# A layer-norm, MLP and memory-recurrence kernel: transposes moved to DMA, the end of the MLP by tiles, two more segments' loads on ScalarE, six last stores

## The chip, the cores and the metric

One NeuronCore of a Trainium2 chip runs the whole program. The metric is the device time of one execution in microseconds; lower is better. TensorE does the matrix products, VectorE and ScalarE the elementwise work, GpSimd some copies, and SyncE, ScalarE and GpSimd issue DMAs.

## The reference

The input `x` has 2048 rows of 1024 bfloat16. It is normalised by rows, and the output is the sum of three things: `x`, a recurrent attention over the normalised rows, and an MLP of the normalised rows.

```python
xn = _layernorm(x, axis=-1)
return x + _A_ref(xn, A_mem0, A_Wq, A_Wk, A_Wv, A_Wo, A_seg_len) + _B_ref(xn, B_w1, B_b1, B_w2, B_b2)

def _B_ref(x, w1, b1, w2, b2):             # w1 1024 x 3584, w2 3584 x 1024
    return gelu(x @ w1 + b1) @ w2 + b2

def _A_ref(x, mem0, Wq, Wk, Wv, Wo, seg_len):   # 32 heads of 128; 64 segments of 32 rows; 8 memory rows
    mem = mem0
    for s in range(n_seg):
        h = jnp.concatenate([mem, xs], axis=1)          # 40 rows
        q, k, v = h @ Wq, h @ Wk, h @ Wv
        p = softmax(where(mask, q @ k.T * scale, -1e9))
        o = (p @ v) @ Wo
        mem = o[:, :M, :]                               # the next segment starts from these rows
        outs.append(o[:, M:, :])
```

The segments depend on one another through the memory rows, so they run in order.

## The kernel before

The program has two stages. The first is the MLP, over four groups of four tiles of 128 rows (`for tg in range(4)`, line 544). The second is the recurrence, over 64 segments (`for s in range(NSEG)`). The order of all instructions is written out by hand: each engine runs its own in the order of the text, and so does each queue of DMAs. The framework adds semaphore waits. It gives the DMAs issued by SyncE and ScalarE eight completion semaphores in turn, and each such DMA waits until the one eight places before it in the program has landed.

**A group of the MLP.** The first product (`first_product`, line 495, matmuls at line 497) makes 28 blocks of 128 hidden columns for the 512 rows of the group from the turned, normalised rows `xnT` (two halves of 512 columns); ScalarE and VectorE apply the gelu and write `gts`. Then, for the first three groups, the `x` tiles of the next group are loaded (`load_x`, line 339), their statistics taken on VectorE (`ln_stats`, line 388, instructions at lines 384 and 386), and a loop over the group's four tiles (line 610) does for each: normalise one tile of the next group (`ln_apply`, line 401, two buffers `ln_xn`), the second product in two halves of 512 columns (28 matmuls each, line 618), two additions on VectorE for each half (lines 625 and 626), the turning of the normalised tile (`turn_x`: eight transposes on TensorE at line 412, two copies out of PSUM at line 417, one on VectorE, one on ScalarE), and the store of the finished tile of `x + MLP` to `R_n` in DRAM (`keep_R`, line 445, on SyncE; on ScalarE for the last four tiles).

After the loop, `keep_xT` (line 427) stores the turned rows for the recurrence (`rows_d`, `rowsL_d`) and has GpSimd copy parts of them, and `turn_R` (line 457, issues at line 484) rearranges `R_n` into `res_d` and `resL_d` by some 56 small DMAs in DRAM, on SyncE for groups 0 and 1, on GpSimd for group 2.

In group 0, between the loads of `x` and the statistics, SyncE also copies 15 of the recurrence's streamed weight units (512 KB each) from the inputs to DRAM scratch (`copies`, by `fetch`, lines 246 and 248) and loads five resident units (`fetch_resident(*EARLY)`).

The last group needs no next one. Its second product runs with all eight results in PSUM: for each of 28 steps `fc`, four tiles by two halves (line 651). Each result starts from a one-row product that adds `b2` (line 644) and a product with the identity that adds `x` (line 645). Slabs that the steps set free get weight units of the recurrence (`fetch_resident`). Eight evictions follow (line 665), four on VectorE and four on ScalarE, and the stores of `R_n`.

**A segment of the recurrence.** Keys, queries and values come from 8 weight units each and half, 48 units, and the output from 16 (`o_product`, line 1027). Of the 64 units of 512 KB, 17 are streamed for each segment through six slabs by SyncE (15 from DRAM, two kept in PSUM), the others stay in SBUF. `put_mem` (line 307) writes the new memory rows into the next segment's input; its VectorE copy at line 324 runs once a segment and marks its end here. The small loads of a segment (its rows, line 286; its residual, lines 1124 and 1150) and the plain stores of its output (line 1218) are on the engine called `loads`:

```python
EARLY_SEGS = 5
loads = nc.scalar if s < EARLY_SEGS else nc.gpsimd
```

In segments 1 to 4 `turn_R` of the last four tiles is put on a list, `small`, of GpSimd DMAs, one or two of which are issued whenever a streamed unit is done. In every fourth segment and the last (`left_o`) the output covers 32 rows more and there are two residual tiles, `res` and `st["resL"]` (in `pd_main`). In the last segment VectorE adds the output to both (line 1184) and twelve stores go out (line 1207), half on SyncE and half on ScalarE.

Of the kernel before, what the change touches and what calls it, by code (L numbers as in the profile page):

```python
# [14 lines left out]
ALU = mybir.AluOpType  # L15
PSUM = bass.MemoryType.PSUM

P = 128
# [6 lines left out]
SEG = 32  # L25
# [3 lines left out]
FC = F // P  # L29
# [8 lines left out]
NX = 24  # L38
NL = SEG - NX
# [9 lines left out]
SCRATCH = 320  # L49
SMALL = 3776  # L50
LEAD = 6
EARLY_SEGS = 5
LEAD_FIRST = 4
SCORES_0 = (6, 6, 6, 5)
SUMS_0 = (4, 4, 4, 4)
# [59 lines left out]
def kernel(  # L115
# [16 lines left out]
    nc = tc.nc  # L132
# [198 lines left out]
    with tc.tile_pool(name="ma", bufs=2) as ma, tc.tile_pool(name="mps", bufs=6, space=PSUM) as mps:  # L331
# [90 lines left out]
        def turn_x(tt, xn, xnT):  # L422
            pT = turned(xn)
            for half in range(2):
                turned_out(tt, pT, half, xnT, nc.scalar.copy if (tt + half) % 2 else nc.vector.tensor_copy)

        def keep_xT(tg, xnT):
            xl = [t[:, 0:512].rearrange("p (g k i t) -> p g k i t", g=2, k=KT, i=GRP) for t in ko_flat]
            for half in range(2):
                nc.sync.dma_start(  # L430
                    out=rows_d[16 * tg:16 * tg + 16, :, 128 * half:128 * half + 128].rearrange("s p c -> p s c"),
                    in_=xnT[half].rearrange("p s k t -> p s (k t)"),
                )
                for g in range(4):
                    nc.gpsimd.tensor_copy(
                        out=xl[g // 2][:, g % 2, 4 * half:4 * half + 4, :, :],
                        in_=xnT[half][:, 4 * g:4 * g + 4, :, NX:SEG].rearrange("p i k t -> p k i t"),
                    )
            for k in range(2):
                nc.sync.dma_start(  # L440
                    out=rowsL_d[4 * tg + 2 * k:4 * tg + 2 * k + 2, :, :].rearrange("g p c -> p g c"),
                    in_=xl[k][:, :, :, :, :].rearrange("p g k i t -> p g (k i t)"),
                )

        def keep_R(ttg, rsb):
            eng = nc.scalar if ttg >= NT - 4 else nc.sync
            eng.dma_start(out=R_n[ttg * P:ttg * P + P, :], in_=rsb[:, :])

        def main_row(slot):
# [94 lines left out]
        for tg in range(4):  # L544
# [53 lines left out]
            if not last:  # L598
                xnT = new_xnT(tg + 1)
                for t in range(4):  # L600
                    xtoks[4 * tg + 4 + t] = load_x(4 * tg + 4 + t)
                if tg == 0:
                    for unit, c in copies.items():
                        fetch(c, unit)
                    fetch_resident(*EARLY)
                for t in range(4):
                    ln_stats(4 * tg + 4 + t)
                ln_sqrt(4 * tg + 4, 4 * tg + 8)
                ln_rstd(4 * tg + 4, 4 * tg + 8)
                for t in range(4):  # L610
                    ttg = 4 * tg + t
                    xn = ln_apply(ttg + 4)
                    rsb = xtoks[ttg]
                    for nb in range(2):
                        cs = slice(nb * 512, (nb + 1) * 512)
                        ps = mps.tile([P, 512], F32, name="ps")
                        for fc in range(FC):
                            nc.tensor.matmul(  # L618
                                ps[:, :],
                                lhsT=gts[fc // 4][:, fc % 4, t * P:(t + 1) * P],  # L620
                                rhs=w2_sb[fc // 2][:, fc % 2, cs],
                                start=(fc == 0),
                                stop=(fc == FC - 1),
                            )
                        nc.vector.tensor_tensor(out=ps[:, :], in0=ps[:, :], in1=b2bc[:, cs], op=ALU.add)
                        nc.vector.tensor_tensor(out=rsb[:, cs], in0=ps[:, :], in1=rsb[:, cs], op=ALU.add)
                        if nb == 1:
                            turn_x(ttg + 4, xn, xnT)
                    keep_R(ttg, rsb)
                keep_xT(tg + 1, xnT)  # L630
                for t in range(4):
                    turn_R(4 * tg + t, nc.gpsimd if tg == 2 else nc.sync)
            else:


                start_stream("xn2")
                start_stream("xn3")
                put_mem(o_sb, nxt["hT"], mps.tile([P, 512], F32, name="ps"), wide=False)
                nc.sync.dma_start(out=d_oL[:, 0:DM], in_=Wo_v[:, h + 1, :])
                pss = [mps.tile([P, 512], F32, name="ps") for _ in range(6)]  # L640
                pss += [mps.tile([P, 512], F32, name="pT", bufs=2) for _ in range(2)]
                for n in range(8):
                    cs = slice((n % 2) * 512, (n % 2 + 1) * 512)
                    nc.tensor.matmul(pss[n][:, :], lhsT=ones[0:1, :], rhs=b2row[0:1, cs], start=True, stop=False)
                    nc.tensor.matmul(
                        pss[n][:, :], lhsT=ident, rhs=xtoks[4 * tg + n // 2][:, cs], start=False, stop=False
                    )
                for fc in range(FC):
                    for t in range(4):
                        for nb in range(2):  # L650
                            nc.tensor.matmul(  # L651
                                pss[2 * t + nb][:, :],
                                lhsT=gts[fc // 4][:, fc % 4, t * P:(t + 1) * P],
                                rhs=w2_sb[fc // 2][:, fc % 2, nb * 512:nb * 512 + 512],
                                start=False,
                                stop=(fc == FC - 1),
                            )
# [16 lines left out]
    with tc.tile_pool(name="late", bufs=1) as late, \  # L674
# [67 lines left out]
        for s in range(NSEG):  # L742
# [435 lines left out]
            for w, r in reversed(list(enumerate(tiles))):  # L1178
                if left_o:
                    o = psX[:, 256 * w:256 * w + 256].rearrange("p (h e) -> p h e", e=32)  # L1180
                else:
                    o = o_sb[:, 0:8, :]
                r_rows = r.rearrange("p (h e) -> p h e", e=32)
                nc.vector.tensor_tensor(out=r_rows, in0=o, in1=r_rows, op=ALU.add)  # L1184
# [11 lines left out]
            if final:  # L1196
                engines = [nc.sync, nc.scalar]
                n = 0
                for w, r in enumerate(tiles):
                    for b in range(2):  # L1200
                        cs = slice(256 * (2 * b + w), 256 * (2 * b + w) + 256)
                        pieces = [(rows, slice(64 * b + m0, 64 * b + m0 + NX))]
                        for sl, row in left_rows:
                            p0 = 64 * b + NL * sl
                            pieces.append((slice(row, row + NL), slice(p0, p0 + NL)))
                        for o, i in pieces:
                            engines[n % 2].dma_start(out=out_flat[o, cs], in_=r[i, :])
# [48 lines left out]
```

## Time and profile before

| | us |
|---|---|
| median of 3 runs | 1818.26 (1816.41 to 4332.87) |
| the profiled execution, its own time | 1811.68 |
| its span, first to last instruction | 1809.9 |
| TensorE busy | 1707.1 |
| VectorE busy | 978.1 |
| ScalarE busy | 687.9 |
| GpSimd busy | 305.2 |
| mean granted TensorE clock | 0.998 |
| MLP, up to the first matmul of the recurrence | 417.0 |
| bytes moved by DMA | 592.07 MB |

The span is one execution, taken by the profiler; times in the text are counted from its first instruction. A group's line on the page gives how often an instruction ran, its busy time in sum, the mean of one in nanoseconds, and the idle time of its engine just before it with what ended that. The chain of waits is followed back from the last instruction, at each step to what released it. In the timeline an entry merges equal instructions that follow one another; a DMA issue on a queue (SPq, ACTq) includes what it waits for. A window's line gives its length, the busy time and number of instructions of TensorE's matmuls, its weight loads, VectorE, ScalarE and GpSimd, and then the granted clock, the DMA engines' share and GB/s.

### The profile page before, as it was taken

The numbers are of one execution on the slowest core, as the hardware profiler recorded it, in microseconds if no ns is written. First come the engines' busy times: TensorE is split into PE (matmuls) and PEld (weight loads), VectorE is DVE, ScalarE is ACT, GpSimd is POOL, SyncE is SP. The second block draws the span as 40 slices with busy tenths as digits, with TensorE's granted clock in tenths as the row PEclk, the third lists the DMA queues.
The fourth block names the chain that finished last, engine by engine and source line by source line (L and its number), as shares of the span: only waits on it lengthen the run. The fifth ranks groups of instructions, "written<-read, shape, count | busy, mean of one in ns | idle before, by whom it ended". The sixth has DMA issues, their size and how long they took to land.

```text
span 1809.9 us, 71522 instructions
## 1 busy us (share of the span) xinstructions
PE 1707.1 (94%) x31173; PEld 893.0 (49%) x31173; DVE 978.1 (54%) x2508; ACT 687.9 (38%) x1700; POOL 305.2 (17%) x595
## 2 busy tenths in 40 slices
PE   8999999998988999999999999999999999999997
PEld 4444444444444545545444555554545454555544
DVE  7657483804554555555555555555555555555554
ACT  6334260702333334333333334343433333434333
POOL 0000000411122211111111212111111111111111
PEclk9999999999999999999999999999999999999999
DMA  9931111769999999999999999999999999999997
GB/s 290 308 100 48 52 48 36 246 225 345 385 371 346 389 377 384 387 377 393 380 373 374 383 395 394 368 398 379 393 385 376 382 370 369 398 393 384 391 396 294
DMA packets 220870, 592.07 MB, mean 327 GB/s; under 512 B 46283, under 2 KB 75995, under 8 KB 220556
## 3 DMA queue, kind: packets, MB, share of 16 engines
q1 hardware_dynamic: 197652, 567.08, 83.5%
q0 software_dynamic: 17184, 17.23, 2.9%
q8 instruction: 244, 4.00, 0.9%
q10 hardware_dynamic: 5720, 3.19, 0.6%
q14 instruction: 70, 0.57, 0.1%
HBM read 573.43 MB, written 28.90 MB: 333 GB/s over the span
## 4 chain that ended last, share of the span: by engine, by line
PE 72%; DMA 13%; issue 6%; ACT 4%; DVE 3%; POOL 1%; ACTq 0%; DVEq 0%; POOLq 0%; SPq 0%
PE acc L769 34%; PE acc L1027 12%; PE ps L497 11%; PE ps L618 8%; DMA u<-Wc_O 7%; DMA u<-Wc_V 3%; PE ps L651 2%; ACT mixed L938 2%; PE acc L978 1%; DMA u<-Wc_Q 1%; PE mixed L886 1%; DVE kq L853 1%; DVE pd_main L951 1%; POOL res_d L486 1%; ACT kq L848 1%
## 5 line engine op out<-in xcount | busy, mean ns | idle before, releaser
L769 PE MATMUL acc<-u,hr_home 128*32 128x512 bf16 x11520 | 760.8, 380 | 15.7 <-issue 6.0
L769 PEld LDWEIGHTS <-hr_home 128*32 128x32 bf16 x12288 | 348.0, 96 | 285.5 <-issue 33.8
L769 PE MATMUL acc<-u,hrL 128*32 128x512 bf16 x2880 | 254.5, 380 | 4.4 <-issue 2.4
L497 PE MATMUL ps<-u 128*128 128x512 bf16 (+1 forms) x920 | 194.4, 373 | 2.0 <-ACT u L417 2.0
L267 DVE TENSOR_SCALAR u<-kept 128x512 uint32<-128x512 uint32 x254 | 163.1, 684 | 51.7 <-PE acc L769 39.2
L821 ACT CAST d_oL<-acc 128x512 bf16<-128x512 f32 x143 | 82.0, 585 | 261.0 <-PE acc L769 254.2
L618 PE MATMUL ps<-u 128*128 128x512 bf16 x672 | 147.0, 379 | 0.0
L1027 PEld LDWEIGHTS <-kq 128*32 128x32 bf16 x3908 | 103.1, 96 | 79.0 <-issue 22.2
L1027 PE MATMUL acc<-u,d_oL 128*32 128x512 bf16 x1944 | 133.9, 381 | 8.5 <-DMA u<-Wc_O 4.7
L497 PEld LDWEIGHTS <-u 128*128 128x128 bf16 x920 | 89.8, 98 | 104.9 <-issue 2.4
L1027 PE MATMUL acc<-u,kq 128*32 128x256 bf16 (+1 forms) x2372 | 117.2, 313 | 16.0 <-DMA u<-Wc_O 13.4
L853 DVE STREAM_TRANSPOSE kq<-kq 128x512 bf16<-128x512 bf16 x128 | 91.0, 711 | 74.8 <-ACT kq L848 72.6
L951 DVE TENSOR_TENSOR pd_main<-kq,mixed 128x320 bf16<-128x320 bf16 x128 | 62.4, 487 | 127.3 <-ACT mixed L938 127.3
L848 ACT CAST kq<-acc 128x512 bf16<-128x512 f32 (+2 forms) x192 | 85.3, 444 | 114.7 <-PE acc L769 85.1
L1218 POOL DMA_DIRECT2D out_dram<-hr_home x172 | 87.2, 514 | 227.3 <-DVE hr_home L1184 226.8
L825 ACT CAST kq<-acc 128x512 bf16<-128x512 f32 x128 | 75.2, 587 | 111.2 <-PE mixed L892 109.9
L769 PEld LDWEIGHTS <-hrL 128*32 128x32 bf16 x3072 | 86.3, 96 | 58.1 <-issue 5.9
L916 DVE TENSOR_TENSOR kq<-kq,mixed 128x96 bf16<-128x96 bf16 (+1 forms) x256 | 38.1, 190 | 125.7 <-ACT kq L906 70.5
L618 PEld LDWEIGHTS <-u 128*128 128x128 bf16 x672 | 65.3, 98 | 77.4 <-DVE g_u L579 0.4
L571 ACT ACTIVATE g_xb<-ps,b1col 128x512 bf16<-128x512 f32 x112 | 76.8, 686 | 55.6 <-PE ps L497 54.7
L938 ACT ACTIVATE mixed<-mixed,small_consts 128x160 f32<-128x160 f32 x256 | 94.2, 368 | 8.4
L1027 PEld LDWEIGHTS <-d_oL 128*32 128x32 bf16 x2592 | 63.8, 96 | 63.8 <-issue 16.1
(132 smaller groups left out, 2015.4 us busy)
## 6 DMA issues: line engine op xcount, KB each, us to landing
u<-Wc_K SPq DMA_DIRECT2D x256, 512.0 KB
u<-Wc_V SPq DMA_DIRECT2D x256, 512.0 KB
u<-Wc_O SPq DMA_DIRECT2D x256, 512.0 KB
u<-Wc_Q SPq DMA_DIRECT2D x192, 512.0 KB
u<-in_B_w_dram SPq DMA_DIRECT2D x28, 512.0 KB
u<-in_A_Wq_dram SPq DMA_DIRECT2D x13, 512.0 KB
u<-in_A_Wv_dram SPq DMA_DIRECT2D x12, 512.0 KB
u<-in_A_Wk_dram SPq DMA_DIRECT2D x9, 512.0 KB
```

Of the source, the lines that this page charges most:

```text
L267: nc.vector.tensor_single_scalar(out=out, in_=in_, scalar=0, op=ALU.bitwise_or)
L497: nc.tensor.matmul(ps[:, SEG * s0:SEG * s1].rearrange("p (s t) -> p s t", t=SEG), lhsT=w1_sb[fb // 2][:, kt, (fb % 2) * P:(fb % 2 + 1) * P ...
L571: nc.scalar.activation(out=xb[:, :], in_=ps[:, :], func=ACT.Identity, bias=b1col[:, fb:fb + 1], scale=1.0)
L618: nc.tensor.matmul(ps[:, :], lhsT=gts[fc // 4][:, fc % 4, t * P:(t + 1) * P], rhs=w2_sb[fc // 2][:, fc % 2, cs], start=(fc == 0), stop=(fc ...
L769: nc.tensor.matmul(o, lhsT=lhs[:, i, :], rhs=m, start=(i == seq[0]), stop=(i == seq[-1]), tile_position=(0, 32 * j),)
L821: cp(out=out, in_=ps.rearrange("p (h e) -> p h e", e=32))
L848: nc.scalar.copy(out=q_home[:, h0:h1, NL:40], in_=ps[:, 32 * h0:32 * h1].rearrange("p (h e) -> p h e", e=32))
L853: nc.vector.transpose(out=home, in_=home)
L938: nc.scalar.activation(out=mixed[:, 160 * b:160 * b + 160], in_=mixed[:, 0:160], func=ACT.Exp, scale=-1.0, bias=off[:, b:b + 1],)
L951: nc.vector.tensor_tensor(out=pdA.rearrange("p c b q -> p b c q"), in0=prA[:, None, :, :].to_broadcast([P, 2, 4, 40]), in1=dd, op=ALU.mult,)
L1027: nc.tensor.matmul(acc[r0:r0 + rows, 0:256 * len(blocks)], lhsT=lhsT, skip_group_check=True, rhs=o_columns(t, k, blocks), start=start, sto ...
L1218: loads.dma_start(out=out_flat[rows, 256 * j:256 * j + 256], in_=res[32 * j:32 * j + NX, :])
```

## The change

It has five parts.

- Tiles 1 to 3 of each next group are turned by DMA: `send_x` issues eight DMA transposes a tile on SyncE, of 32 rows by 512 columns each, straight from `ln_xn` into `xnT`, ahead of the tile's second product. Tile 0 is still turned by TensorE, after its second product.
- The stores of `R_n` for tiles 0 to 2 of a group go to ScalarE. The copies of the streamed units and the five early loads of group 0 stand behind the loop over the tiles on SyncE.
- In the last group the left half of each result no longer gets `x` by a product with the identity; VectorE adds it at the eviction. The last four of the 28 steps run tile by tile.
- `EARLY_SEGS` is 7: segments 5 and 6 have their small loads and plain stores on ScalarE.
- In the last segment the two sums are written side by side into `d_oL`, and six stores of 512 columns take the place of twelve of 256.

```diff
-EARLY_SEGS = 5
+EARLY_SEGS = 7
...
+        def send_x(t, xn, xnT):
+            for i in range(4):
+                for half in range(2):
+                    nc.sync.dma_start_transpose(
+                        out=xnT[half][:, 4 * t + i, :, :],
+                        in_=xn[SEG * i:SEG * i + SEG, 512 * half:512 * half + 512],
+                    )
...
         def keep_R(ttg, rsb):
-            eng = nc.scalar if ttg >= NT - 4 else nc.sync
+            eng = nc.scalar if ttg >= NT - 4 or ttg % 4 < 3 else nc.sync
...
                 for t in range(4):
                     xtoks[4 * tg + 4 + t] = load_x(4 * tg + 4 + t)
-                if tg == 0:
-                    for unit, c in copies.items():
-                        fetch(c, unit)
-                    fetch_resident(*EARLY)
...
                     xn = ln_apply(ttg + 4)
+                    if t > 0:
+                        send_x(t, xn, xnT)
...
-                        if nb == 1:
+                        if nb == 1 and t == 0:
                             turn_x(ttg + 4, xn, xnT)
                     keep_R(ttg, rsb)
+                if tg == 0:
+                    for unit, c in copies.items():
+                        fetch(c, unit)
+                    fetch_resident(*EARLY)
                 keep_xT(tg + 1, xnT)
...
-                    nc.tensor.matmul(
-                        pss[n][:, :], lhsT=ident, rhs=xtoks[4 * tg + n // 2][:, cs], start=False, stop=False
-                    )
-                for fc in range(FC):
-                    for t in range(4):
-                        for nb in range(2):
+                    if n % 2:
+                        nc.tensor.matmul(
+                            pss[n][:, :], lhsT=ident, rhs=xtoks[4 * tg + n // 2][:, cs], start=False, stop=False
+                        )
+                steps = [(fc, t) for fc in range(FC - 4) for t in range(4)]
+                steps += [(fc, t) for t in range(4) for fc in range(FC - 4, FC)]
+                for fc, t in steps:
+                    for nb in range(2):
...
-                    if fc % 2:
+                    if t == 3 and fc % 2:
                         fetch_resident(f"w2_{fc // 2}")
-                    if fc % 4 == 3:
+                    if t == 3 and fc % 4 == 3:
                         fetch_resident(f"gT{fc // 4}")
...
-                    cp = nc.scalar.copy if n % 2 else nc.vector.tensor_copy
-                    cp(out=xtoks[4 * tg + n // 2][:, cs], in_=pss[n][:, :])
+                    x = xtoks[4 * tg + n // 2][:, cs]
+                    if n % 2:
+                        nc.scalar.copy(out=x, in_=pss[n][:, :])
+                    else:
+                        nc.vector.tensor_tensor(out=x, in0=pss[n][:, :], in1=x, op=ALU.add)
...
-                nc.vector.tensor_tensor(out=r_rows, in0=o, in1=r_rows, op=ALU.add)
+                to = d_oL[:, 256 * w:256 * w + 256].rearrange("p (h e) -> p h e", e=32) if final else r_rows
+                nc.vector.tensor_tensor(out=to, in0=o, in1=r_rows, op=ALU.add)
...
-                for w, r in enumerate(tiles):
-                    for b in range(2):
-                        cs = slice(256 * (2 * b + w), 256 * (2 * b + w) + 256)
+                for b in range(2):
+                    cs = slice(512 * b, 512 * b + 512)
...
-                        for o, i in pieces:
-                            engines[n % 2].dma_start(out=out_flat[o, cs], in_=r[i, :])
-                            n += 1
+                    for o, i in pieces:
+                        engines[n % 2].dma_start(out=out_flat[o, cs], in_=d_oL[i, 0:512])
+                        n += 1
```

More of the change, by code (lines that the diff above doesn't have):

```diff
@@ L644 @@
                     nc.tensor.matmul(pss[n][:, :], lhsT=ones[0:1, :], rhs=b2row[0:1, cs], start=True, stop=False)
-                    nc.tensor.matmul(
-                        pss[n][:, :], lhsT=ident, rhs=xtoks[4 * tg + n // 2][:, cs], start=False, stop=False
-                    )
-                for fc in range(FC):
-                    for t in range(4):
-                        for nb in range(2):
[L651 to L657, printed above, removed]
-                    if fc % 2:
+                    if n % 2:
[6 more added lines that the diff above has]
+                    for nb in range(2):
+                        nc.tensor.matmul(
+                            pss[2 * t + nb][:, :],
+                            lhsT=gts[fc // 4][:, fc % 4, t * P:(t + 1) * P],
+                            rhs=w2_sb[fc // 2][:, fc % 2, nb * 512:nb * 512 + 512],
+                            start=False,
+                            stop=(fc == FC - 1),
+                        )
+                    if t == 3 and fc % 2:
                         fetch_resident(f"w2_{fc // 2}")
-                    if fc % 4 == 3:
+                    if t == 3 and fc % 4 == 3:
                         fetch_resident(f"gT{fc // 4}")
@@ L1198 @@
                 n = 0
-                for w, r in enumerate(tiles):
-                    for b in range(2):
-                        cs = slice(256 * (2 * b + w), 256 * (2 * b + w) + 256)
[L1202 to L1205, printed above, removed]
-                        for o, i in pieces:
-                            engines[n % 2].dma_start(out=out_flat[o, cs], in_=r[i, :])
-                            n += 1
+                for b in range(2):
+                    cs = slice(512 * b, 512 * b + 512)
+                    pieces = [(rows, slice(64 * b + m0, 64 * b + m0 + NX))]
+                    for sl, row in left_rows:
+                        p0 = 64 * b + NL * sl
+                        pieces.append((slice(row, row + NL), slice(p0, p0 + NL)))
+                    for o, i in pieces:
+                        engines[n % 2].dma_start(out=out_flat[o, cs], in_=d_oL[i, 0:512])
+                        n += 1
             elif left_o:
```

## The prediction

> **What bounds the kernel now.** I read the page first, then the chain of waits over the first 430 us, then SyncE's queue beside VectorE's timeline around the second token group, then the chain and the windows around 565 us, and the tail. The engine rows and the DMA row of the page:
>
> ```profile
> PE 1707.1 (94%) x31173; PEld 893.0 (49%) x31173; DVE 978.1 (54%) x2508; ACT 687.9 (38%) x1700; POOL 305.2 (17%) x595
> ...
> DMA  9931111769999999999999999999999999999997
> ```
>
> TensorE is busy 94% of the span. The DMA engines are full from the tenth slice on (the recurrence) and nearly idle from the fourth to the seventh (most of the MLP). So in the MLP, which the change mostly edits, TensorE alone should set the time, and only its gaps and extra work can be saved. The chain of waits, second token group:
>
> ```profile
> 161.86 12.09 PE ps L618 x56
> 173.94 0.45 PE pT L412 x8
> ...
> 211.54 0.46 PE pT L412 x8
> ...
> 212.03 0.59 ACT u L417
> ...
> 212.66 48.51 PE ps L497 x224
> ```
>
> A tile's second product takes 12.09 us, its eight transposes 0.45 us; at the end of a group the transposes and ScalarE's copy lie between the last product (211.54) and the next group's first (212.66), 1.12 us. SyncE's queue, where the change rearranges most:
>
> ```profile
> 58.91 2.71 SPq L246 DMA_DIRECT2D Wc_O<-in_A_Wo_dram  x4
> ...
> 83.80 2.65 SPq L248 DMA_DIRECT2D u<-in_A_Wk_dram  x2
> 87.60 26.44 SPq L447 DMA_DIRECT2D R_n<-u  x4
> 114.13 2.55 SPq L430 DMA_DIRECT2D rows_d<-u  x2
> ...
> 155.58 1.87 SPq L344 DMA_DIRECT2D u<-in_A_x_dram  x4
> ```
>
> The 20 half-megabyte issues (15 weight copies in DRAM, 5 loads) hold SyncE from 58.91 to 87.54, 28.6 us, in time when it has nothing urgent. After the group, rows_d and the 56 small DMAs of turn_R fill it from 114.13 until it reaches the x loads of the third group at 155.58. VectorE takes these x tiles up soon after:
>
> ```profile
> 164.92 1.28 DVE L384 BATCH_NORM_STATS2 ln_stats<-u 128x6 f32<-128x512 bf16 x2
> ...
> 171.20 0.55 DVE L403 TENSOR_SCALAR ln_xn<-u,ln_mv,ln_rstd 128x1024 bf16<-128x1024 bf16 x1
> ```
>
> and TensorE transposes the result at 173.94. That chain has only some 9 us to spare. In the recurrence, segment 6 (from the write of its memory rows at line 324 to the next) takes 25.64 us, where later segments of its kind (10, 14, 18, 22) take 20.0 to 21.3. The chain and two windows:
>
> ```profile
> 561.01 1.24 DMA hr_home<-res_d
> 562.25 5.07 DMA pd_main<-resL_d
> ...
> 567.75 0.41 DVE hr_home L1184
> ```
> ```profile
> 564.00:568.00 4.00, 1.17 (x24) 0.34 (x16) 0.59 (x2) 0.00 (x0) 0.00 (x0) 1.00 0.86 328
> 568.00:572.00 4.00, 3.64 (x46) 1.65 (x50) 2.53 (x6) 1.17 (x2) 1.09 (x2) 0.73 0.60 170
> ```
>
> GpSimd, behind its small DMAs, issues segment 5's residual loads late (562.25, 0.7 us before the memory write; in segment 9 it is 6.1 us before); TensorE idles 3.05 us and then runs 3.4 us at half clock. The tail on SyncE:
>
> ```profile
> 1804.46 1.10 SPq L1207 DMA_DIRECT2D out_dram<-hr_home  x3
> 1805.97 1.42 SPq L1207 DMA_DIRECT2D out_dram<-pd_main  x3
> ```
>
> **The change part by part.** *Transposes by DMA.* In each of three groups, tiles 1 to 3 lose 8 TensorE transposes: 6 inner tiles x 0.45 = 2.7 us, and 3 group ends x 1.12 = 3.36 us, together 6.0 us. The copies out of PSUM that also go (9 of 0.59 us on ScalarE, 9 of 0.41 on VectorE) were hidden except at the group ends. In their place stand 24 DMA transposes a group on SyncE, each 32x512. For the last tile they can be issued once VectorE has finished the tile before (two adds of 0.7 us) and the normalisation (0.55), 2.1 us into a product of 12.09; so 10 us remain for eight issues and a landing. The trace has no DMA transpose. The nearest rows are other small SyncE DMAs, 0.6 us of issue: 8 x 0.6 + 2 for the landing = 6.8 us, hidden. The other bound is the pace at which the DRAM copies land, 1.83 us each (SyncE's waits from 64.6 to 90.2, 14 copies). I take the near row: -6.0 us; the far bound is a rival. The Trainium skill (VectorE: DVE Perf Modes, The three transpose paths) gives 1309 ns for a 128x128 crossbar transpose by DMA, the same number of elements, and so speaks against this edit: my estimate from it is 10.5 us for eight, 2.5 us late at each of three ends, 7.5 us more in the sum. No run here shows it yet.
>
> *Stores of R_n on ScalarE.* Nine issues of 0.36 us, each waiting for VectorE's last add of its tile. Behind them on ScalarE stands nothing until the next group's first activation, 12 us after the third: free. GpSimd's copies of the transposed rows stay hidden in the first product.
>
> *The copies and early loads behind the loop.* Their data is needed only after 313 us, so they cost nothing themselves. What stands behind them on SyncE does: rows_d, turn_R, then the third group's x loads. They now start at the last R_n store, some 0.6 us ahead of the old rows_d, and each waits, as the built program has it, for the landing of the DMA eight places before it. At the measured 28.6 us for the block, the x issue goes from 155.58 - 0.9 to 183.3. From there: 2.4 us to the first tile, then VectorE's 6.8 us from the first statistics (164.92) to the normalised tile (171.75), so 192.5. TensorE, running 2.0 us earlier by then (two transposed tiles and one group end), finishes tile 0 at 171.9 and next in its order stand the eight transposes of tile 0 of the next group, which are still on TensorE. It stalls 20.6 us. Afterwards the clock: after the 3.05 us gap above it lost 1.7 us, at the kernel's start 2.8; I take 2.0. Sum +22.6. Bounds: were only issue time to count (15 x 0.6 + 5 x 0.33 = 10.7 us), the stall would be 2.7 us without clock loss; if rows_d and the first turn_R also wait behind the last landings, 24 + 3. I take the measured block, since the eight-deep waits are unchanged. Only the third group's loads are hit: the second's are ahead of the copies, the fourth's have no copies ahead.
>
> *Last group.* Four x matmuls go; a pair there takes 0.64 us: -1.3 us. At 365 us the clock is halved for 3.4 us (loss 1.7), after the slow one-row matmuls; with a shorter stretch I count half: -0.8 (bounds 0 and -1.7). The tile-by-tile end lets six of eight evictions finish early, but the first recurrence product waits for the last ScalarE and VectorE eviction: 1.16 us idle before, about 0.8 after (0.7 of eviction plus 0.1), -0.35. The half-megabyte fetch into the slab freed by step 25 is issued 2.6 us later; DMA share is 0.61 from 415 to 420, so 0.3 (up to 1.3).
>
> *Loads of segments 5 and 6 on ScalarE.* They leave GpSimd's backlog. Segment 6 should fall from 25.64 to the 20.3 or so of its kind: -5; ScalarE gets three and six issues more, and a landing took 6.3 us on that queue in segment 1, so I take -4.5 (bounds -5.3 and +3, if the issues delay the evictions TensorE waits for).
>
> *Six stores.* Three issues less on SyncE, whose last now ends at 1805.6 instead of 1807.4: -1.6 (0 to -2).
>
> Sum: 22.6 - 6.0 - 2.1 - 0.35 + 0.3 - 4.5 - 1.6 = +8.4 us. The profiled execution took 1811.68 us (span 1809.9 and 1.8 around it), so 1820.1; the runs' median, 1818.26, lies 6.6 above it, so I predict 1826.7.
>
> **Rivals.** (1) *No stall, faster.* If the copies, starting into empty DMA engines, leave SyncE after little more than issue time, the x issue is at 165.4 and the stall 2.7 us: -11.5, so 1806.8. It decides from an x issue before about 163 (no stall at all, 1804). For it: the copies met a backlog at 58.9. Against: nine of them issued at once there, and only then the waits of 1.4 to 3 us began. (2) *Transposes late, slower.* At 1.83 us each, 24 take 44 us against a window of 36; the last lands near 122 where the group ends at 111: 11 us late, three times, +33 on top: 1860. Against: 32 KB each, a sixteenth of the copies' bytes. (3) *Segments 5 and 6 lose.* The loads on ScalarE sit before evictions and wait there; with +3 in place of -4.5: 1834. Against: segments 1 to 3 run so now, within 2 us of their later kind. That the change does not do what it says is excluded by the built program: 72 DMA transposes, 6 stores and the late copies stand in it.
>
> **How the numbers follow.** Forecast 0.68 (own range 1814 to 1836), rival 1 0.14, rival 2 0.11, rival 3 0.07. The range 1800 to 1850 takes in rivals 1 and 3 and leaves rival 2 out. Two per cent, 36 us, is about what a measurement of this kernel can tell from no change: only rival 2 passes it (from 1854.6): slower 0.09, faster 0.01, within 0.90.
>
> **What would show it.** In the changed profile: SyncE's x issue of the third group near 183; VectorE's statistics at about 186 instead of 165; a TensorE gap of some 20 us before the transposes of the second group's tile 0, ended by ln_xn, with half clock behind it; no gap at the three group ends; segment 6 near 20.5 us; three stores a queue at the end. The prediction is wrong if TensorE runs on through 172 to 192 us, or if it waits at the group ends for DMA transposes.

## The result and the profile after

The changed kernel takes 1834.55 us (median of 6 runs, 1831.31 to 1842.17) against 1817.41 us for the kernel before; the ratio is 1.0101, 95% interval 1.0078 to 1.0125. It is slower by 14 to 23 us, inside the 2% that was called no change. One of the six runs of the kernel before took 4332.87 us; it is not in the ratio. The forecast was 1826.7 in a range of 1800 to 1850. The profiled execution after took 1838.78 us, 4 above its median (span 1837.1), and the one before 1811.68, 6 below its own. So stages are compared below, each by itself, and not the two spans.

The rows of the page that answer to those shown of before:

```profile
PE 1711.3 (93%) x31097; PEld 895.4 (49%) x31097; DVE 975.3 (53%) x2499; ACT 683.4 (37%) x1691; POOL 301.4 (16%) x586
...
PEclk9999799999999999999999999999999999999999
DMA  9454121657999999999999999999999999999998
```

TensorE runs 76 matmuls fewer and is busy 4 us longer: part of its work ran at a lower clock, in the fifth slice, where the granted clock shows a 7. The DMA engines' work has moved from the second slice to the third and fourth; the recurrence is as full as before.

The chain of waits over the first 460 us, from the end of the first group to the third:

```profile
111.72 0.66 issue
112.38 1.02 PE ps L506 x4
...
150.94 2.53 SPq L449
...
189.84 2.83 DMA u<-in_A_x_dram
192.70 1.30 DVE ln_stats L384 x2
...
198.99 0.56 DVE ln_xn L403
199.59 1.03 PE pT L412 x8
200.63 38.71 PE ps L625 x168
```

Before, the same stretch was TensorE from end to end, but for ScalarE's copies at the group ends. Now 39 us of the chain (150.94 to 189.84) are SyncE's issues, `rowsL_d` at line 449 and the small ones of `turn_R` at line 493, left out here; the `x` load of the third group stands behind them. SyncE's queue, each entry with what it waited for:

```profile
77.29 35.08 SPq L431 DMA_TRANSPOSE u<-ln_xn  x24
113.21 0.34 SPq L456 DMA_DIRECT2D R_n<-u  x1
113.60 2.65 SPq L246 DMA_DIRECT2D Wc_O<-in_A_Wo_dram  x4
...
137.72 2.95 SPq L248 DMA_DIRECT2D u<-in_A_Wk_dram  x2
141.89 8.95 SPq L439 DMA_DIRECT2D rows_d<-u  x2
...
189.84 1.86 SPq L344 DMA_DIRECT2D u<-in_A_x_dram  x4
```

The 15 copies and five early loads hold it from 113.6 to 141.9, 28.3 us; then the two `rows_d` issues take 8.95 where before they took 2.55. The windows before, in and after the stall (length; busy time and count of TensorE's matmuls, its weight loads, VectorE, ScalarE, GpSimd; granted clock; DMA share; GB/s):

```profile
160.00:173.00 13.00, 13.00 (x62) 5.85 (x60) 3.45 (x10) 3.85 (x6) 0.00 (x0) 1.00 0.13 37
173.00:200.00 27.00, 0.70 (x7) 0.41 (x6) 6.76 (x15) 0.30 (x1) 0.00 (x0) 0.60 0.22 65
200.00:215.00 15.00, 15.00 (x62) 6.55 (x61) 4.31 (x8) 0.59 (x1) 0.79 (x2) 0.82 0.14 37
```

TensorE stands still for 26.3 us (173.30 to 199.59), no engine is busy for more than about a quarter of the window and DMA moves 65 GB/s; afterwards it runs at half clock until 205.5, so that the 168 matmuls of 36.26 us take 38.71.

The stages, from the profiles, in us. S1 is the second product of the second group with its group end (the stall's place), "other S" those of the first and third, "last" the last group's second product up to the first matmul of the recurrence, "end" what follows the last write of memory rows; a second product is counted from the start of the last matmul ahead of it. "Before, again" is a second profile of the same kernel, taken with the experiments.

| | first products | other S | S1 | last | MLP | segment 0 | segment 6 | segments 7-62 | end |
|---|---|---|---|---|---|---|---|---|---|
| before | 205.9 | 103.0 | 51.2 | 56.9 | 417.0 | 34.6 | 25.6 | 1192.9 | 28.4 |
| before, again | 207.0 | 103.0 | 51.2 | 55.2 | 416.4 | 34.9 | 21.3 | 1199.3 | 29.0 |
| after | 207.3 | 99.7 | 78.5 | 57.6 | 443.0 | 36.7 | 20.0 | 1200.2 | 26.1 |

The MLP is 26 us longer: 27.3 in S1, 1.4 in the first products and 0.7 in the last group, and 3.3 back from the other groups. Of the recurrence, segment 6 and the end are shorter as foreseen.

### The profile page after: what moved, and what is told of

Read it like the earlier page. It is cut to its first block, busy times and chain, and to the rows that moved or that the text cites. A ratio compares the mean times of both kernels' runs of the same rounds, so it can differ in the third digit from the quotient of the medians.

```text
span 1837.1 us, 71457 instructions
## 1 busy us (share of the span) xinstructions
PE 1711.3 (93%) x31097; PEld 895.4 (49%) x31097; DVE 975.3 (53%) x2499; ACT 683.4 (37%) x1691; POOL 301.4 (16%) x586
## 4 chain that ended last, share of the span: by engine, by line
PE 72%; DMA 15%; DVE 4%; ACT 3%; issue 3%; SPq 2%; ACTq 0%; POOL 0%; DVEq 0%; POOLq 0%
PE acc L785 35%; PE acc L1043 12%; PE ps L506 10%; DMA u<-Wc_O 9%; PE ps L625 7%; DMA u<-Wc_V 4%; PE ps L664 2%; SPq L493 2%; ACT mixed L954 1%; PE acc L994 1%; DMA u<-Wc_Q 1%; PE mixed L902 1%; DVE kq L869 1%; DVE pd_main L967 1%; ACT kq L864 1%
## 5 line engine op out<-in xcount | busy, mean ns | idle before, releaser
L1043 PE MATMUL acc<-u,d_oL 128*32 128x512 bf16 x1944 | 132.7, 381 | 11.7 <-DMA u<-Wc_O 6.8
L506 PEld LDWEIGHTS <-u 128*128 128x128 bf16 x920 | 90.1, 99 | 106.3 <-issue 3.9
```

The source lines that it names most:

```text
L506: nc.tensor.matmul(ps[:, SEG * s0:SEG * s1].rearrange("p (s t) -> p s t", t=SEG), lhsT=w1_sb[fb // 2][:, kt, (fb % 2) * P:(fb % 2 + 1) * P ...
L1043: nc.tensor.matmul(acc[r0:r0 + rows, 0:256 * len(blocks)], lhsT=lhsT, skip_group_check=True, rhs=o_columns(t, k, blocks), start=start, sto ...
```

## Experiments

The theory: the whole loss is the third group's `x` load behind the copies, the early loads, `rows_d` and `turn_R` on SyncE, and without it the change would gain. The rivals: the DMA transposes themselves cost time, or the gains of the other parts are smaller than the sum had them. Each kernel was compared with runs of the kernel before on the same chip.

**Copies back at their old place (`e1_copies_back`).**

```diff
                     xtoks[4 * tg + 4 + t] = load_x(4 * tg + 4 + t)
+                if tg == 0:
+                    for unit, c in copies.items():
+                        fetch(c, unit)
+                    fetch_resident(*EARLY)
```

> The changed kernel, but with the 15 weight copies and 5 early loads of group 0 where they were before (between the x loads and the statistics). Theory 1 (the copies push the third group's x loads from 155.6 to 189.8 us, TensorE waits 26.3 us for the normalised tile and then runs 5.4 us at half clock, about 29 us in all): that gap is gone. In its place the DMA transposes of group 0 wait on SyncE behind the copies until about 87.5; 24 issues of 1.27 us end near 118, 7 us after the group's last product at 111.3, so about -29 + 7 = -22: 1813, ratio 0.997 to 0.999. Rival A (the DMA transposes themselves cost the time, by their issue and their traffic): the gap at the end of group 0 grows and nothing else falls, 1830 or more. Rival B (the recurrence has become slower; segments 7 to 62 took 7.2 us more in the profiled execution): those segments stay 7 us longer than before.

Measured: 1819.58 against 1813.4 us, ratio 1.0033 [1.0008, 1.0058], some 6 us more than expected. S1 is 49.3: the stall has gone from the third group. But the first group's DMA transposes now wait behind the copies (the first is issued at 90.1), and TensorE waits for them at the end of that group, 111.27 to 122.95, 11.7 us where 7 were expected, with 10.2 us of half clock in the records (from 115.7 to 126.0, so 3 us of it after the wait). Its chain of waits:

```profile
111.31 0.71 DVE ps L636
...
112.74 1.14 SPq L431
...
120.33 2.38 DMA u<-ln_xn
122.95 17.17 PE ps L506 x72
```

Each issue takes 1.24 us here too, one after the other, though nothing else stands on SyncE. Moving the copies was therefore no mishap beside the transposes: with the transposes on SyncE the copies cannot stay in one block ahead of them.

**Copies in three parts (`e2_copies_split`).** Behind each group's `x` loads, 7, 7 and 6 of the 20.

```diff
+                for _ in range(7):
+                    if waiting:
+                        waiting.popleft()()
...
-                if tg == 0:
-                    for unit, c in copies.items():
-                        fetch(c, unit)
-                    fetch_resident(*EARLY)
```

> The changed kernel, with the 20 issues cut into three parts of 7, 7 and 6, each behind the x loads of a group, where SyncE has some 17 us before the first DMA transpose of that group. Theory 1: no gap at the third group's normalised tile, DMA transposes on time except for 0.3 to 1 us at each group end: -29, so about 1805, ratio 0.993 to 0.995. Rival A: as slow as the changed kernel or up to 5 us faster, 1829 to 1835. Rival B: the recurrence stays 7 us longer, 1812.

Measured: 1807.9 against 1813.4 us, ratio 0.9962 [0.9942, 0.9982]. No stall is left in the MLP but one of 1.16 us in the last group (`e6_early_mem` below); the three second products are 49.93, 49.51 and 49.21 us against 51.82, 51.19 and 51.19 before. The same work, with nothing but the place of 20 issues changed, is faster than the kernel before, and the stall was the whole loss. Which part of the change the 0.4% belongs to is another question: see `e5_no_transposes` and `e3_segs_stores`.

**`x` loads of the third group on GpSimd (`e4_x_on_pool`).**

```diff
-            nc.sync.dma_start(out=xt, in_=x_flat[tt * P:(tt + 1) * P, :])
+            eng = nc.gpsimd if 8 <= tt < 12 else nc.sync
+            eng.dma_start(out=xt, in_=x_flat[tt * P:(tt + 1) * P, :])
```

> The changed kernel, but the four x loads of the third group are issued by GpSimd, whose queue is empty then, so they no longer stand behind the copies and turn_R on SyncE; copies and DMA transposes stay where the change put them. Theory 1: the loads land about 130 us, long before VectorE's statistics at 164; no gap, -29: about 1805, ratio 0.993 to 0.995. Rival A or any other cost of the late copies: the gap stays or moves, 1825 to 1835.

Measured: 1821.77 against 1813.4 us, ratio 1.0053 [1.0035, 1.0071], so the expected 1805 was missed. The tiles come in time (statistics at 164.5), and the stall is not gone but moved. SyncE's next entries behind `turn_R` are the DMA transposes, in the chain

```profile
191.60 0.62 SPq L494
192.99 1.23 SPq L432
...
221.14 2.37 DMA u<-ln_xn
223.75 16.43 PE ps L507 x68
```

24 of them in a row from 192.99, and TensorE waits from 210.24 to 223.75, 13.5 us. So everything late on SyncE counts, not the `x` loads alone; taking one of them off the queue saved half of the stall.

**No DMA transposes, old place of the copies (`e5_no_transposes`).** The last group, the loads and the six stores stay changed.

```diff
-                    if t > 0:
-                        send_x(t, xn, xnT)
...
-                        if nb == 1 and t == 0:
+                        if nb == 1:
                             turn_x(ttg + 4, xn, xnT)
...
-            eng = nc.scalar if ttg >= NT - 4 or ttg % 4 < 3 else nc.sync
+            eng = nc.scalar if ttg >= NT - 4 else nc.sync
```

> The changed kernel with the first two parts undone: all four tiles turned by TensorE, R_n stored from SyncE, the copies of group 0 where they were before. Left of the change: the last group, segments 5 and 6 on ScalarE, six stores. If the stages add up: group ends as before (51.2 to 51.8 us a second product), segments 1 to 6 shorter by 6 to 7, tail by 2.4, the last group by 2.6 where no half clock falls on it and longer by 0.7 where it does, segment 0 longer by 1.4: 1804 to 1807, ratio 0.994 to 0.996. Against the copies cut in three it should be about 5.5 us slower, the worth of the transposes in the MLP. Rival (the DMA transposes cost something outside the MLP, in the recurrence): equal to or faster than the copies cut in three.

Measured: 1811.33 against 1816.4 us, ratio 0.9966 [0.9946, 0.9987]. Second products as before (51.82, 51.19, 51.19), MLP 417.0. It was expected to be some 5.5 us slower than the copies in three parts, whose MLP takes 409.7 us; but the two ratios, 0.9966 and 0.9962, differ by 0.7 us, each known to some 4 us, which speaks for the rival. So what the DMA transposes save in the MLP is not seen in the whole time, and what becomes of it was not found.

**Memory rows written early in the last group (`e6_early_mem`).** This starts from the copies in three parts. The reason for it is in the timeline of TensorE after the change, at the start of the last second product (an entry ends with the idle time before it and what ended that):

```profile
387.59 0.38 PE L655 MATMUL ps<-b2row,ones 1*128 1x512 bf16 x1
389.13 0.37 PE L655 MATMUL ps<-b2row,ones 1*128 1x512 bf16 x1 [1.16 <-DVE hr_home L324]
```

The sixth PSUM buffer is held by `put_mem`, whose copy at line 324 stands on VectorE behind the last gelu. The four products with the identity used to cover that time; with them gone TensorE waits, and in this profile 6.8 us of half clock follow, where the first profile of before has 3.4.

```diff
             for fb in range(FC):
+                if last and fb == 14:
+                    put_mem(o_sb, nxt["hT"], mps.tile([P, 512], F32, name="ps"), wide=False)
...
-                put_mem(o_sb, nxt["hT"], mps.tile([P, 512], F32, name="ps"), wide=False)
```

> The copies cut in three, and put_mem of the last group moved from the end of the first product to its fifteenth block, so that the sixth result's PSUM buffer is free when the one-row products reach it. If the wait of 1.16 us for VectorE's copy at line 324 has eaten the worth of the four removed matmuls: that gap is gone and the stretch from the first product to the recurrence is 53.1 us in place of 54.3, without half clock; ratio to before lower by 0.0006 than the copies cut in three, too little to see in the time. Rival (another wait takes its place, as the gelu of the last block): the stretch stays at 54.3.

Measured: 1806.15 against 1816.4 us, ratio 0.995 [0.9927, 0.9972]. The wait is gone, and "last" is 52.8 us against 54.3 without this edit, as expected; it is 57.6 in the changed kernel and 55.2 to 56.9 before. Only the 1.5 us are the edit's. The rest of the distance to 57.6 is half clock, and that varies: after the same wait of 1.2 to 1.3 us the records show 6.8 us of it in four profiles, 3.4 in two and none in two (the copies in three parts and `e4_x_on_pool`); with the old last group one profile of five has 3.4 there and the others none. This is the shortest of all medians, by the ratios some 27 us below the changed kernel's and 0.5% below the kernel before; against the copies in three parts alone the intervals overlap.

**Plain order of the last steps (`e7_plain_steps`).** The copies in three parts, and the 28 steps as before.

```diff
-                steps = [(fc, t) for fc in range(FC - 4) for t in range(4)]
-                steps += [(fc, t) for t in range(4) for fc in range(FC - 4, FC)]
+                steps = [(fc, t) for fc in range(FC) for t in range(4)]
```

> The copies cut in three, with the 28 steps of the last group all in the old order (four tiles in each step), VectorE adding x as in the change. If the later release of the last slabs makes segment 0 longer: segment 0 falls from 36.0 to 34.6 us, and the gap before the first product of the recurrence grows from 0.67 to about 1.2: net -0.9 us, not to be seen in the time. Rival (something else has lengthened segment 0): it stays near 36.0.

Measured: 1807.68 against 1816.4 us, ratio 0.9951 [0.9933, 0.9969]. The gap before the first recurrence product is 1.16 us again (0.67 with the steps by tiles), which is the half microsecond that was counted for it; in the whole time it cannot be seen. Segment 0 stays long, 35.8 us, so the slabs that are freed later are not what lengthened it by 1 to 2 us; with no transposes (`e5_no_transposes`) it is 36.3, with the old last group 34.6 to 34.9. It belongs to the last group's edits, by what way is open.

**Loads of segments 5 and 6, and six stores: together and alone.** On the kernel before. Together (`e3_segs_stores`):

```diff
-EARLY_SEGS = 5
+EARLY_SEGS = 7
...
-                nc.vector.tensor_tensor(out=r_rows, in0=o, in1=r_rows, op=ALU.add)
+                to = d_oL[:, 256 * w:256 * w + 256].rearrange("p (h e) -> p h e", e=32) if final else r_rows
+                nc.vector.tensor_tensor(out=to, in0=o, in1=r_rows, op=ALU.add)
...
-                            engines[n % 2].dma_start(out=out_flat[o, cs], in_=r[i, :])
+                        engines[n % 2].dma_start(out=out_flat[o, cs], in_=d_oL[i, 0:512])
```

> The kernel before with only two parts of the change: the loads of segments 5 and 6 on ScalarE, and the six last stores. By the profiles, segment 6 falls from 25.6 to about 20 us and segments 1 to 6 together by about 5.9, the tail by about 2.2: 1809.5, ratio 0.995 to 0.997. Rival B (these loads disturb what follows and segments 7 to 62 become 7 us longer): 1816 to 1818, ratio 0.999 to 1.000.

Measured: 1806.65 against 1813.4 us, ratio 0.9951 [0.9933, 0.9969], from four runs. The loads alone (`e9_segs_only`):

```diff
-EARLY_SEGS = 5
+EARLY_SEGS = 7
```

> The kernel before, with the loads of segments 5 and 6 on ScalarE and nothing else. Theory (the gain of those loads is carried through to the end): segments 1 to 6 shorter by some 2 us in the profile (129.55 us stood with the loads and the stores changed together, 131.46 in the second profile of before) and the median 4 to 6 us under the kernel before, of the 7 that the loads and stores gave together. Rival (the recurrence is set by its 383 GB/s of DMA, so that a saving in segments 5 and 6 is given back in segments 7 to 62): recurrence in the profile between 1391 and 1398 us as in all profiles so far, median within 2 us of the kernel before.

Measured: 1814.05 against 1815.17 us, ratio 0.9999 [0.9979, 1.0018]: the rival's median, not the theory's. The stores alone (`e10_stores_only`), with the lines above but the first pair.

> The kernel before, with the two last sums side by side and six stores, and nothing else. Theory: the end (after the last write of memory rows) falls from 28.4 to 29.0 us to about 25.5 to 26.5, and the median by 2 to 3 us. Rival (the end of the stores is set by the landing of the last one, whatever their number): the end stays at 28 to 29 us, the median within 1 us of the kernel before.

Measured: 1810.04 against 1815.17 us, ratio 0.9986 [0.9961, 1.0012], not clear of no change; the end is 26.2 us against 28.4 and 29.0, as the theory has it. Multiplied, the two alone come to 0.9985, where both together were measured at 0.9951 from four runs; the intervals are too wide to call that a difference.

**The second profile of before (`e8_before_again`)**, without an edit, was taken to see how much of a stage belongs to one execution.

> The kernel before, looked at once more. Segments 7 to 62 took 1192.9 us in its first profile and 1195.8 to 1204.3 in five others with the same code there. If this is the spread of one execution: again a value between 1193 and 1204, at random. If the other kernels are really longer there: again 1191 to 1195.

Measured: 1812.72 us. Segment 6 is 21.3 us long here, not 25.6, with 1.6 us of idle TensorE at its start instead of 3.05 and no half clock. With all profiles laid side by side this sorts itself out. With five early segments, segment 6 took 25.6, 21.3, 23.5, 25.4 and 24.4 us and began with a gap of 1.6 to 3.8 us in each; with seven it took 19.7 to 22.2, mean 20.5, in nine profiles. So the edit takes 3.6 us out of segment 6 on average. But segments 7 to 62 took 1191 to 1204 us from profile to profile, with either setting. Their mean is 1196.8 us in the five profiles and 1200.4 in the nine, so the 3.6 us may be given back there; with such a spread this is not shown.

**The change's part in the MLP alone,** with the loads of segments 5 and 6 on GpSimd and twelve stores: with the copies in three parts (`e11_mlp_split`) and behind the loop as in the change (`e12_mlp_late`). In both, against the changed kernel or the one in three parts:

```diff
-EARLY_SEGS = 7
+EARLY_SEGS = 5
...
-                        engines[n % 2].dma_start(out=out_flat[o, cs], in_=d_oL[i, 0:512])
+                            engines[n % 2].dma_start(out=out_flat[o, cs], in_=r[i, :])
```

> The changed kernel with the 20 copies and early loads in three parts behind each group's x loads, the loads of segments 5 and 6 back on GpSimd and the twelve stores back: the change's work in the MLP without its stall. Theory (gains add): the MLP's end at 408 to 411 us against 416 to 417 in the kernel before, second products 49.9, 49.5 and 49.2, and the median 5 to 7 us under the kernel before; with the 7 us of the loads and stores the whole would then have given 13, but 5.5 us were measured for the split kernel. Rival (the MLP's saving is partly given back in the first segments, where DMA is busy all the time): the recurrence 3 us or more longer than 1393, the median 0 to 3 us under the kernel before.

Measured: 1815.48 against 1815.17 us, ratio 0.9995 [0.997, 1.0019], though the MLP is 412.8 us in the profile, 3.5 to 4.1 shorter (408 to 411 were expected; 6.8 us of half clock fell into the last group). The median is the rival's. Its longer recurrence the profile does not show (1391.2 us), but that was the fastest of the twelve executions.

> The change's work in the MLP as it is, with the copies behind the loop, but the loads of segments 5 and 6 on GpSimd and the twelve stores. Theory (stall of 26 to 29 us at the third group, less what the transposes save, and nothing given back): first recurrence product at about 443 us; median 26 us above the kernel before, that is 7 to 9 above the changed kernel, if loads and stores are worth that by themselves. Rival (loads and stores worth only the 2.5 us at the end): median about 19 to 21 us above the kernel before.

Measured: 1850.64 against 1815.17 us, ratio 1.0191 [1.0154, 1.0229], that is 28 to 42 us above the kernel before and, by the medians, 16 above the changed kernel: more than theory or rival had it. The stall is the same (S1 78.35), and the recurrence begins at 442.2 us, as expected. Segment 6 begins as in the kernel before; its chain in the copies-in-three-parts kernel, and below it that of the kernel before with the loads of segments 5 and 6 on ScalarE:

```profile
560.58 4.82 DMA pd_main<-resL_d
...
565.84 0.42 DVE hr_home L1201
566.26 0.04 issue
566.31 5.17 PE acc L786 x60
```
```profile
560.64 0.86 PE acc L769 x16
...
561.69 5.51 PE acc L769 x100
```

In the first, TensorE's segment begins when the residual has come; in the second the residual is not on the chain.

What stays open: how much of the loads' 3.6 us and of the transposes' 5.5 us reaches the end. The split kernel's 0.4% is no more than the loads and stores gave without any change in the MLP (0.9951), and the MLP's part without them gives nothing (0.9995). On the kernel before the loads give nothing that can be measured (at most 4 us); on the changed MLP, taking loads and stores away cost 16 us by the medians, of which the profiles of the two show 5.6 in segments 1 to 6 and 1.7 at the end. The recurrence is full with DMA, and its total lay between 1390 and 1398 us in 13 profiles and at 1404 in the last kernel's. A rule by which the first segments' state decides the later ones was not found. Single spans of one kernel also lie up to 10 us from its median, so no single profile decides this.

## Why the prediction was right or wrong

The direction, the mechanism and the place were right. The stall is before tile 0's transposes at the end of the second group's first tile, it ends with `ln_xn`, half clock follows, and no other place in the MLP waits as long. Point by point:

- *The block of 20 issues* was put at 28.6 us and took 28.3, although the DMA engines were nearly idle when it began. Rival 1, that it would run at little more than issue time, falls.
- *The `x` issue* was put at 183.3 and came at 189.84, the statistics at 192.7 instead of 186, the stall was 26.3 us instead of 20.6, and the half clock cost 3.0 (2.45 in the product, 0.58 in the transposes) instead of 2.0. With S1's normal 49.5 the term is 29.0 against 22.6. The step that failed is the sentence that moves what stands behind the block without changing its length: the two `rows_d` issues were taken along at their 2.55 us, and took 8.95. These 6.4 us are nearly the whole lateness of the `x` issue, 6.5. A row for it stood in the trace of before, at the place where the first group's two issues meet DMA engines busy to 1.02 (window 42 to 56), and it was not read:

```profile
44.08 9.98 SPq L430 DMA_DIRECT2D rows_d<-u  x2
```

The bound of 24 + 3 allowed for such a wait and was not taken; the 26.3 + 3.0 that came even pass it.
- *Transposes by DMA* were to give 6.0 us. The second products gave 5.55 (the copies in three parts: 1.89, 1.68 and 1.98), and the first products that follow are 0.2 to 0.4 longer, 0.9 in sum: 4.7 net. In the whole time none of it shows (`e5_no_transposes`). The price of a DMA transpose was wrong: 0.6 us was taken from the small DMAs, and the trace has

```profile
L431 SPq DMA_TRANSPOSE u<-ln_xn x72: 1162/1237/2226, 77.3 to 335.7; - x72
```

least, median and largest, in ns. Eight take 10.3 us, and the last of the first group leaves SyncE at 112.37, 0.65 after TensorE's last product. It was to be wholly hidden; it costs the 0.66 us of "issue" in the chain above. The Trainium skill (VectorE: DVE Perf Modes, The three transpose paths) gives 1309 ns for this size, and by pace the trace agrees with it; the 2.5 us late at each end that was estimated from it was too much, since the first four matmuls need only the half that comes first, and the next begin at 113.57, 1.2 us after the last issue has ended. Rival 2's 1.83 us each did not come.
- *Last group*: -2.5 was foreseen in all, and "last" came out at 57.6 us against 56.9 and 55.2. The matmuls were counted as time on the path, but they covered VectorE's way to line 324. Their 1.3 us turned into 1.16 us of waiting, and the half clock that was to become shorter was twice as long in this profile. `e6_early_mem` shows the wait: without it the stretch is 1.5 us shorter, and 2.4 us shorter than in the second profile of before, where no half clock fell on it either. The half clock itself is not a fixed price, as said there. Segment 0, for which 0.3 us were counted, came out some 2 us longer (36.7 against 34.6 and 34.9); `e7_plain_steps` shows that the late fetch is not the reason.
- *Loads of segments 5 and 6*: -4.5 foreseen, -3.6 in segment 6 over 14 profiles (20.0 us in the changed kernel's, 20.5 foreseen). The later segments of its kind took 20.0 to 20.5 us, not up to 21.3. Part of the 5 us had been one execution's share of a wait that varies. What of it arrives at the end is open, as said. Rival 3 is not borne out.
- *Six stores*: -1.6 foreseen; the three issues on SyncE after the change end at 1834.8, 2.3 us before the span does, and the end is 2.1 to 2.8 us shorter with the stores alone.

So the sum of +8.4 became +17 to +18. The MLP's share was put at +14.2 and came to +26: 6.4 from the stall, 3 from the last group, 1.3 from the transposes, and 1 within what first and second products differ anyway. The rest of the program was put at -5.8. If the MLP is 26 us longer in every run, it came to -8 or -9 by the medians; the profiles of the two kernels do not show that (1392.9 us from the first matmul of the recurrence before, 1394.1 after), and no run explains it. In the MLP the errors all lay on the slow side, 12 us together; that the time stayed so near the forecast, and inside its own 1814 to 1836, is in part luck.

## What to carry to other kernels

A block of DMA issues that "has no hurry" delays everything behind it in its queue, and the first issues behind it may themselves take longer while its transfers run. Follow the queue to the next item with a deadline, price the items between by how they run beside busy DMA engines, and if the deadline is short, deal the block out in parts behind items that have none; here that turned 1% slower into 0.4% faster. A shorter stage is not yet a shorter program: without the stall the MLP ended at 408.8 to 412.8 us instead of 416.4 to 417.0, and no run shows that gain in the whole time. Before a matmul is removed, ask what it covered: the next wait on TensorE may be as long as the work that went. And an unmeasured operation is priced by the nearest operation of its own kind; a small DMA was no measure for a transpose.

## What the runs showed of the hardware

The half clock comes in whole steps: the records of it (but the one that the program's end cuts short) are 3.41, 6.83, 10.24, 13.65 and 27.31 us long, one, two, three, four and eight times 3.41; the three longest go with idle times of 11.7, 13.5 and 26.3 us. With a short one the length varies: a wait of 1.2 to 1.3 us in the last group was met by 6.83, by 3.41 or by none. After the 26.3 us stall it began 4.9 us after TensorE's last matmul and ended 5.9 us after its next first one. The Trainium skill (TensorE: Matmul & The Clock Gate, What's actually happening) has a free-running window of 3413 ns; the trace agrees with its length.

DMA transposes issued one after the other on SyncE left it at 1.24 us each (median) in the changed kernel and in the two where they came late, and TensorE went on 2.4 to 2.6 us after the issue of the one that it waited for had begun.

The issue of a DMA has no fixed price on SyncE. The two `rows_d` issues (512 KB each) took 8.9 to 10.7 us where the DMA engines were busy (share 1.02 in the kernel before from 42 to 56 us, 0.95 in the changed one from 142 to 151) and 2.2 to 3.5 us elsewhere (0.79 in the kernel before from 114 to 117). In the changed kernel it is the second of the two that stands for 8.46 us, and the wait for the DMA eight places before it is an entry of its own that ends ahead of it, at 142.34. The profile puts 8.0 us of it down to ScalarE's activation `g_sg`, but ScalarE's part of these rows, the copy of tile 0 at line 417, was done at 77 us. What holds the issue, a full queue or something else, was not tried.
